# Moving the attention output step behind the gate arithmetic in a fused attention and SwiGLU kernel

## The chip, the cores and the metric

The kernel runs on one core of a Trainium2 chip. The core has five engines that work at the same time, each with its own instruction queue that it goes through in order: TensorE (PE in the profile; its weight loads are the row PEld), VectorE (DVE), ScalarE (ACT), GpSimd (POOL) and SyncE (SP, which here only issues transfers). They wait for each other through semaphores. Matmuls write to PSUM, a small memory of banks; DVE and ACT read the results from there.

The metric is the device time of one execution in microseconds (us). For the kernel before, three runs gave a median of 332.81 us, from 332.54 to 332.84.

## The reference

Two stages are computed one after the other. The first is attention with a hash mask, for 4 batches, 8 heads, 768 positions and 64 dimensions per head:

```
q_bits = (q @ proj > 0)                  # 6 bits per position; k_bits likewise
mask   = bucket(q_bits) == bucket(k_bits)
scores = where(mask, q @ k^T / 8, -1e9)
attn   = softmax(scores)                 # row sum + 1e-9 in the divisor
x      = attn @ v                        # heads side by side: 3072 tokens x 512
```

The second is a feed-forward block with RMS norm and a gate:

```
rms = sqrt(mean(x*x) + 1e-6)
xn  = x / rms * rms_g
out = (silu(xn @ w_gate) * (xn @ w_val)) @ w_out     # 512 -> 1536 -> 512
```

## The kernel before

The work is cut into 8 units of 384 query rows: batch u // 2, half u % 2. A unit has 8 heads, and a head takes 3 steps of scores. The program is written as a list of slots, NS = 24 for each unit and 8 * NS = 192 in all. A slot t issues `scores` (line 328) for step t + 1 on TensorE, `probs` (line 343, the exponential on ScalarE) for step t, and then every step that the list `plan[t]` holds, in the order in which the steps were put in with `at`. Each engine gets its instructions in this order, so the order of the list is the order of the queues. There is no other planner behind it.

These are the steps in the plan that matter here:

- `av` (line 352) multiplies the probabilities of a head with v into `o_ps`. A pair of heads shares one `o_ps` tile, and the pool that holds it has one buffer, so the next pair can start only when `o_ps` has been read. For head number n of the order, `av` runs in slots 3n + 4 and 3n + 5.
- `o_step` calls `attn_out` (line 368). Once a pair of heads is complete, in the slot of its last `av`, DVE reads `o_ps` into `otmp` (line 374), takes the reciprocal of the row sums, `rcp` (line 379), and POOL multiplies both to `x` (line 381). POOL then squares `x` into `sq` (line 387). In units 0 and 7 the last pair has all of this on DVE, with three instructions that square and sum at once (line 390).
- `s_step` calls `sumsq` (line 395), a DVE sum of `sq` into `ssp`. It comes five slots after `o_step`, and two slots after it for the last pair of a unit.
- `norm` (line 415) sums `ssp` on DVE (`ss`, line 408), lets POOL compute `rstd` (line 412), and scales `x` to `xn` on DVE (line 423). It stands in slot 4 of the next unit's 24 slots. `turn_x` (line 425) turns `xn` on TensorE (`x_ps`) and writes it back through DVE (`xnT`).
- `gate` and `value` (lines 449 and 458) are the first two matmuls of the feed-forward block, each in two parts of two matmuls. After the second part of `gate`, ScalarE takes a tanh of `g_ps` into `t` (line 455). After the second part of `value`, DVE forms `a` from `t` and `g_ps` (line 464) and `ht` from `a` and `v_ps` (line 465). Those two reads free the banks of `g_ps` and `v_ps`.
- `project` (line 471) is the last matmul, into `y_ps`; `store` copies it out and sends it off.
- `hash_one` (line 281) computes the mask bits of a head pair (matmuls into `d_ps`, DVE `bits`, eight transfers), and `turn_dve` (line 182) turns q and k on DVE. `v_mean` (line 313) makes `cvb`.

The tiles `g_ps`, `v_ps`, `y_ps`, `x_ps`, `d_ps` and `m_ps` all come from one pool of three PSUM banks (`bank`, line 83), used in turn. A `value` that follows a `gate` needs the bank that was used three tiles earlier.

The feed-forward work of unit u is spread over the 24 slots of unit u + 1 by `spread` (line 732): first the nine `project` pieces of unit u - 1 with the turns of `xn`, then the 48 pieces of `gate` and `value`. The plan is filled in this order: early steps, then `av`, `o_step` and `s_step` of all pairs in the loop from line 687 on, then `norm` and the pieces of `spread` with the inserted `hash_one` and `v_mean`, and last the turns, casts and loads (line 787 on). So within one slot DVE meets `otmp`, `rcp` and a row sum ahead of that slot's `a` and `ht`, and these ahead of `bits` and the turns.

A slot with number s has the place s % 24 in its unit. `o_step` of the pairs 0 to 3 stands at places 8, 14, 20 and, in the next unit's slots, 2. `s_step` stands at 13, 19, 1 and 4.

Of the kernel before, what the change touches and what calls it, by code (L numbers as in the profile page):

```python
# [8 lines left out]
FP32 = mybir.dt.float32  # L9
# [24 lines left out]
def kernel(  # L34
# [12 lines left out]
    nc = tc.nc  # L47
# [9 lines left out]
    spool = ctx.enter_context(tc.tile_pool(name="spool", bufs=2))  # L57
# [268 lines left out]
    x, xn, xnT = {}, {}, {}  # L326
# [41 lines left out]
    def attn_out(u, hp, eng=nc.gpsimd):  # L368
        b = u // 2
        if hp == 0:  # L370
            x[u] = xpool.tile([128, 3, DMODEL], FP32, name="x")
        o = ot.pop((u, hp))
        tmp = spool.tile([128, 3, 2, 66], FP32, name="otmp")
        nc.vector.tensor_add(  # L374
            tmp[:, :, :, 0:65], o[:, :, :, 0:65],
            cvb[b % 2][:, 2 * hp : 2 * hp + 2, 0:65].unsqueeze(1).to_broadcast([128, 3, 2, 65]),
        )
        r = spool.tile([128, 3, 2, 1], FP32, name="rcp")
        nc.vector.reciprocal(r, tmp[:, :, :, 64:65])  # L379
        xd = x[u][:, :, 128 * hp : 128 * hp + 128]  # L380
        eng.tensor_mul(  # L381
            xd.rearrange("p c (h d) -> p c h d", h=2), tmp[:, :, :, 0:64],
            r.to_broadcast([128, 3, 2, 64]),
        )
        sq = spool.tile([128, 3, 128], FP32, name="sq")
        if eng is nc.gpsimd:
            eng.tensor_mul(sq, xd, xd)  # L387
            return sq
        for c in range(3):
            nc.vector.tensor_tensor_reduce(  # L390
                out=sq[:, c], in0=xd[:, c], in1=xd[:, c], scale=1.0, scalar=0.0,
                op0=ALU.mult, op1=ALU.add, accum_out=ssp[u % 2][:, hp, c : c + 1],
            )

    def sumsq(u, hp, sq):
        nc.vector.tensor_reduce(  # L396
            out=ssp[u % 2][:, hp, :], in_=sq, op=ALU.add, axis=AX.X
        )
# [156 lines left out]
    NS = 24  # L555
# [5 lines left out]
    def at(w, s, f, *a):  # L561
        plan[NS * w + s].append(lambda: f(*a))
# [116 lines left out]
    sqs = {}  # L679

    def o_step(u, hp, *eng):
        sqs[u, hp] = attn_out(u, hp, *eng)

    def s_step(u, hp):
        sumsq(u, hp, sqs.pop((u, hp)))

    for n, (u, h) in enumerate(order):
        t = 3 * n + 4 - ((u, h) == (0, H - 1))
        for part in range(2):
            at(0, t + part, av, u, h, part)  # L690
        if h % 2:
            if (u, h) == (0, H - 1):

                at(0, t + 1, o_step, u, h // 2, nc.vector)
                at(0, t + 1, norm_scale, u)
                at(0, t + 1, nc.vector.tensor_scalar_mul, gcol, gcol, float(DMODEL) ** 0.5)
                at(0, t + 2, hash_only, 1, 1)
                at(0, t + 2, hash_signs, 1, 1)
                at(0, t + 2, norm, u)
                at(0, TX-1, norm_third, u, 2, nc.scalar.mul)  # L700
                at(0, TX + 1, send_pair, 1, 1)
                for c in range(3):
                    at(0, TX, turn_x, u, c, c == 2)
                continue
            if (u, h) == order[-1]:
                at(0, t + 1, o_step, u, h // 2, nc.vector)
                continue
            at(0, t + 1, o_step, u, h // 2)
            at(0, t + (6 if h < 7 else 3), s_step, u, h // 2)

    hole = []

# [19 lines left out]
    def spread(t0, n, pieces):  # L732
        fixed = [SCORES + (AV if (t - 1) % 3 < 2 else 0) for t in range(t0, t0 + n)]
        extra = [(t, *inserts.pop(t)) for t in range(t0, t0 + n) if t in inserts]
        total = sum(fixed) + sum(p[0] for p in pieces) + sum(e[1] for e in extra)
        i, done = 0, 0
        for s in range(n):
            done += fixed[s]
            while i < len(pieces):
                weight, whole, steps = pieces[i]  # L740
                full = done + weight // 2 > total * (s + 1) // n
                if extra and whole and t0 + s >= extra[0][0] and (full or extra[0][1] > MEAN):
                    _, weight, *step = extra.pop(0)
                    at(0, t0 + s, *step)
                    done += weight
                    continue
                if full:
                    break
                done += weight
                for delay, *step in steps:  # L750
                    at(0, t0 + s + delay, *step)
                i += 1
        for _, _, *step in extra:
            at(0, t0 + n - 1, *step)
        assert i == len(pieces)

    for u in range(7):
# [11 lines left out]
        for i in range(9):  # L769
            c, n = divmod(i, 3)  # L770
            steps = [(0, project, u - 1, c, 4 * n, 4 * n + 4)]
# [6 lines left out]
                ]  # L778
        spread(t0, NS, pieces + gates)
    for t, (_, *step) in inserts.items():  # L780
        at(0, t, *step)

    def behind_norm(t):

        return t - t % NS + 7 if 1 <= t % NS < 7 else t

    for (b, hp), (load, kturns, qturns, _) in spots.items():
# [3 lines left out]
        for w, turns in (("k", kturns), ("q", qturns)):  # L791
            for i, t in enumerate(turns):
                at(0, t, turn_dve, b, hp, w, i, len(turns))
            t = turns[-1] + 1
            at(0, t if (b, hp) == (1, 2) else behind_norm(t), cast_pool, b, hp, w)
        t = 54 if (b, hp) == (1, 2) else behind_norm(qturns[-1] + 2)
# [66 lines left out]
```

## Time and profile before

| what | value |
|---|---|
| median of the runs | 332.81 us |
| the profiled execution's own time | 333.62 us |
| its span, first to last instruction | 331.8 us |
| TensorE busy | 325.6 us |
| VectorE busy | 238.5 us |
| ScalarE busy | 227.1 us |
| GpSimd busy | 163.4 us |
| `otmp`, 32 instructions of 559 ns | 17.9 us |
| `sq` on POOL, 30 of 826 ns | 24.8 us |
| row sums `ssp`, 30 of 529 ns | 15.9 us |

The profile is of one execution, and its span leaves out 1.8 us of that execution's time. Busy time of TensorE is a sum over pipelined instructions whose ends are modelled, so it is the starts of matmuls that tell how fast TensorE goes: two matmuls in a row that start one matmul's time apart leave no gap. Times in the views of the trace count from the start of the span.

### The profile page before, as it was taken

The page shows a single profiled execution, that of the slowest core. Times are in us where ns is not written, and L with a number is a line of the kernel's source. Part 1 is how long each engine was busy: PE and PEld are TensorE (multiplying, and loading weights), DVE is VectorE, ACT ScalarE, POOL GpSimd, SP SyncE. Part 2 cuts the span into 40 slices and gives each one's busy share as a digit, 9 for nine tenths or more (in the row PEclk, how much of TensorE's full clock was granted, in tenths as well). Part 3 has the DMA queues.
Part 4 walks back from the last instruction along what each step waited for, and adds up shares of the span by engine and source line. Part 5 has one row for each costly group of instructions (what it writes and reads, how often), then busy time and mean ns, then how long its engine had stood idle before and what let it go on. Part 6 is the DMA issues. An engine that isn't in the chain of part 4 may idle for free.

```text
span 331.8 us, 7843 instructions
## 1 busy us (share of the span) xinstructions
PE 325.6 (98%) x2998; PEld 196.8 (59%) x2999; DVE 238.5 (72%) x496; ACT 227.1 (68%) x331; POOL 163.4 (49%) x210
## 2 busy tenths in 40 slices
PE   9999999999999999999999999999999999999995
PEld 3576666656565565656566565655656566665553
DVE  5887876859887668867888478886767356675860
ACT  6899887666777667775778667776767767744331
POOL 3999759965974734625574523556461111111000
PEclk9999999999999999999999999999999999999999
DMA  7942999987139554332816036001000010002002
GB/s 212 355 154 68 231 214 197 184 164 141 68 55 162 110 118 94 62 87 76 168 18 134 36 89 120 6 3 68 34 4 2 28 63 9 0 2 95 3 0 96
DMA packets 79613, 30.93 MB, mean 93 GB/s; under 512 B 64908, under 2 KB 76632, under 8 KB 79576
## 3 DMA queue, kind: packets, MB, share of 16 engines
q1 hardware_dynamic: 75672, 25.65, 32.8%
q0 software_dynamic: 3680, 4.72, 8.4%
q8 instruction: 23, 0.38, 0.5%
q14 instruction: 14, 0.11, 0.1%
q10 hardware_dynamic: 224, 0.07, 0.1%
HBM read 28.32 MB, written 6.29 MB: 104 GB/s over the span
## 4 chain that ended last, share of the span: by engine, by line
PE 93%; DVE 2%; ACT 1%; POOL 1%; DMA 1%; issue 0%; SPq 0%; POOLq 0%
PE s_ps L335 19%; PE v_ps L447 18%; PE g_ps L447 18%; PE y_ps L476 17%; PE o_ps L360 10%; PE t_ps L155 2%; PE d_ps L215 2%; PE d_ps L235 2%; PE x_ps L430 2%; PE z_ps L543 1%; DVE xn L423 1%; ACT psb L347 1%; PE y_ps L495 1%; DMA qL<-in_q_dram 1%; PE m_ps L319 0%
## 5 line engine op out<-in xcount | busy, mean ns | idle before, releaser
L347 ACT ACTIVATE psb<-s_ps,ebias 128x768 f16<-128x768 f32 x192 | 167.7, 899 | 21.1 <-PE s_ps L335 20.0
L335 PE MATMUL s_ps<-QK 128*128 128x384 f16 (+1 forms) x384 | 93.6, 326 | 1.2 <-ACT psb L347 1.1
L455 ACT ACTIVATE t<-g_ps 128x384 f32<-128x384 f32 x96 | 47.1, 491 | 54.5 <-PE g_ps L447 53.8
L447 PE MATMUL g_ps<-xnT,wg 128*128 128x384 f16 x384 | 82.7, 326 | 0.0
L447 PE MATMUL v_ps<-xnT,wv 128*128 128x384 f16 x384 | 81.8, 326 | 0.4 <-DVE a L464 0.2
L464 DVE SCALAR_TENSOR_TENSOR a<-t,g_ps 128x384 f32<-128x384 f32 x96 | 52.8, 550 | 26.3 <-ACT t L455 24.9
L476 PE MATMUL y_ps<-wo,ht 128*128 128x512 f16 x276 | 68.1, 379 | 0.0
L381 POOL TENSOR_TENSOR x<-otmp,rcp 128x384 f32<-128x384 f32 x30 | 25.1, 836 | 86.4 <-DVE rcp L379 86.0
L465 DVE SCALAR_TENSOR_TENSOR ht<-a,v_ps 128x384 f16<-128x384 f32 x96 | 53.2, 554 | 11.6 <-PE v_ps L447 3.1
L360 PEld LDWEIGHTS <-psb 128*128 128x128 f16 x1152 | 51.9, 97 | 15.7 <-issue 1.3
L360 PE MATMUL o_ps<-vl,psb 128*128 128x65 f16 x1152 | 55.8, 193 | 0.0
L335 PEld LDWEIGHTS <-QK 128*128 128x128 f16 (+1 forms) x384 | 34.5, 98 | 34.6 <-issue 9.2
L447 PEld LDWEIGHTS <-wv 128*128 128x128 f16 x384 | 35.3, 97 | 22.7 <-issue 2.0
L447 PEld LDWEIGHTS <-wg 128*128 128x128 f16 x384 | 34.7, 97 | 20.9 <-DVE xnT L436 0.4
L476 PEld LDWEIGHTS <-ht 128*128 128x128 f16 x276 | 24.8, 98 | 22.4
L488 ACT COPY ysb<-y_ps 128x512 f32<-128x512 f32 x23 | 13.5, 585 | 19.7 <-PE y_ps L476 19.7
L387 POOL TENSOR_TENSOR sq<-x 128x384 f32<-128x384 f32 x30 | 24.8, 826 | 2.4
L207 POOL CAST QK<-qT 64x768 f16<-64x768 f32 x20 | 16.4, 821 | 17.7 <-DVE qT L194 17.1
L374 DVE TENSOR_TENSOR otmp<-o_ps,cvb 128x390 f32<-128x390 f32 x32 | 17.9, 559 | 10.0 <-PE o_ps L360 9.8
L396 DVE TENSOR_REDUCE ssp<-sq 128x3 f32<-128x384 f32 x30 | 15.9, 529 | 7.9 <-POOL sq L387 7.8
L207 POOL CAST QK<-kT 64x768 f16<-64x768 f32 x20 | 16.4, 820 | 9.0 <-DVE kT L194 7.1
L423 DVE TENSOR_SCALAR xn<-x,rstd 128x512 f16<-128x512 f32 x23 | 15.8, 739 | 6.8 <-POOL rstd L412 6.8
(83 smaller groups left out, 283.1 us busy)
## 6 DMA issues: line engine op xcount, KB each, us to landing
vn<-in_v_dram SPq DMA_DIRECT2D x16, 384.0 KB
out_dram<-ysb SPq DMA_DIRECT2D x23, 256.0 KB
qL<-in_q_dram SPq DMA_DIRECT2D x40, 96.0 KB
kL<-in_k_dram SPq DMA_DIRECT2D x40, 96.0 KB
kn<-in_k_dram SPq DMA_DIRECT2D x5, 384.0 KB
qn<-in_q_dram SPq DMA_DIRECT2D x5, 384.0 KB
wg<-in_moe_w_gate_dram POOLq DMA_DIRECT2D x2, 768.0 KB, 9.5
wv<-in_moe_w_val_dram POOLq DMA_DIRECT2D x2, 768.0 KB, 11.8
```

What stands on the lines that cost most here:

```text
L207: nc.gpsimd.tensor_copy(QK[b, 2 * hp + hh, "h"][0:64, o : o + S], src[64 * hh : 64 * hh + 64, :])
L335: nc.tensor.matmul(ps[:, j, 0:HALF], QK[b, h, "h"][rows, S + jt * 128 : S + (jt + 1) * 128], QK[b, h, "h"][rows, half * HALF : (half + 1) ...
L347: nc.scalar.activation(psb[u, h][:, 2 * ch : 2 * ch + 2, :], sps.pop((u, i))[:, :, 0:HALF], AF.Exp, bias=ebias, scale=ESCALE,)
L360: nc.tensor.matmul(o[:, c, hh, 0:65], psb[u, h][:, jt, c * 128 : (c + 1) * 128], vls[b % 2][:, h, 2 * (jt % 3) + jt // 3 if b in PARITY el ...
L381: eng.tensor_mul(xd.rearrange("p c (h d) -> p c h d", h=2), tmp[:, :, :, 0:64], r.to_broadcast([128, 3, 2, 64]),)
L387: eng.tensor_mul(sq, xd, xd)
L423: mul(xn[u][:, c, :], x[u][:, c, :], rstds[u][:, c : c + 1])
L447: nc.tensor.matmul(ps, w[:, kt, fs], xnT[u][:, kt, :], start=(kt == 0), stop=(kt == 3))
L455: nc.scalar.activation(t, fbank[u, ft, "g_ps"], AF.Tanh, scale=0.5)
L464: nc.vector.scalar_tensor_tensor(out=a, in0=t, scalar=1.0, in1=g, op0=ALU.add, op1=ALU.mult)
L465: nc.vector.scalar_tensor_tensor(out=ht[u][:, ft, :], in0=a, scalar=0.5, in1=vv, op0=ALU.mult, op1=ALU.mult)
L476: nc.tensor.matmul(y, ht[u][:, ft, c * 128 : (c + 1) * 128], wo[:, ft, :], start=(ft == 0), stop=(ft == NF - 1),)
```

## The change

In the loop that plans `av`, `o_step` and `s_step`, steps in slots below 48, and those at places 2 and 4 of a unit, are put into the plan as before. All others are kept in a list and put in after the pieces of `spread` and the inserted steps, but still ahead of the turns, casts and loads. So in these slots `otmp`, `rcp`, `x`, `sq` and the row sums come behind that slot's `a`, `ht`, `bits` and `cvb` in the queues. TensorE's own order stays as it was.

The last pair of units 1 to 6 no longer squares on POOL. Its `s_step` instead issues the three DVE instructions that square and sum in one, reading `x`.

```
-        sq = spool.tile([128, 3, 128], FP32, name="sq")
-        if eng is nc.gpsimd:
+        if eng is nc.gpsimd and hp < 3:
+            sq = spool.tile([128, 3, 128], FP32, name="sq")
             eng.tensor_mul(sq, xd, xd)
             return sq
+        if eng is nc.vector:
+            sumsq_dve(u, hp)
+
+    def sumsq_dve(u, hp):
+
+        sq = spool.tile([128, 3, 128], FP32, name="sq")
+        xd = x[u][:, :, 128 * hp : 128 * hp + 128]
         for c in range(3):
             nc.vector.tensor_tensor_reduce(
...
     def s_step(u, hp):
-        sumsq(u, hp, sqs.pop((u, hp)))
-
+        sq = sqs.pop((u, hp))
+        if sq is None:
+            sumsq_dve(u, hp)
+        else:
+            sumsq(u, hp, sq)
+
+    late = []
...
-            at(0, t + 1, o_step, u, h // 2)
-            at(0, t + (6 if h < 7 else 3), s_step, u, h // 2)
+
+            steps = [(t + 1, o_step), (t + (6 if h < 7 else 3), s_step)]
+            for s, step in steps:
+                if s < 2 * NS or s % NS in (2, 4):
+                    at(0, s, step, u, h // 2)
+                else:
+                    late.append((s, step, u, h // 2))
...
     for t, (_, *step) in inserts.items():
         at(0, t, *step)
+
+    for t, *step in late:
+        at(0, t, *step)
```

## The prediction

> **What bounds the kernel now.** I read the page's busy times and clock first, then the chain of work that ended last, then the costliest groups.
>
> ```profile
> PE 325.6 (98%) x2998; PEld 196.8 (59%) x2999; DVE 238.5 (72%) x496; ACT 227.1 (68%) x331; POOL 163.4 (49%) x210
> PEclk9999999999999999999999999999999999999999
> PE 93%; DVE 2%; ACT 1%; POOL 1%; DMA 1%; issue 0%; SPq 0%; POOLq 0%
> L447 PE MATMUL v_ps<-xnT,wv 128*128 128x384 f16 x384 | 81.8, 326 | 0.4 <-DVE a L464 0.2
> ```
>
> TensorE carries 93% of the chain at full clock. The change gives it no work and takes none away, so it can only move the gaps between matmuls. The group row shows almost none (0.4 us), yet that idle time is counted against modelled, overlapping ends. I therefore measure gaps from start to start. The chain in order of time gives the price of a group without a gap:
>
> ```profile
> 79.30 0.86 PE y_ps L476 x4
> 81.14 0.65 PE v_ps L447 x4
> ```
>
> A 384-column matmul costs 0.1625 us (0.65 / 4), a 512-column one 0.216 us. The timeline from slot 48 on (span 67 us) was then searched for starts that lie further apart. Here are slots 163 to 165, with some lines left out:
>
> ```profile
> 252.30 0.49 PE L447 MATMUL v_ps<-xnT,wv 128*128 128x384 f16 x2
> ...
> 252.50 0.49 ACT L455 ACTIVATE t<-g_ps 128x384 f32<-128x384 f32 x1 [0.73 <-PE g_ps L447]
> ...
> 253.22 0.49 PE L447 MATMUL v_ps<-xnT,wv 128*128 128x384 f16 x2
> 253.42 0.56 DVE L374 TENSOR_TENSOR otmp<-o_ps,cvb 128x390 f32<-128x390 f32 x1 [0.40 <-PE o_ps L360]
> 253.55 0.81 PE L447 MATMUL g_ps<-xnT,wg 128*128 128x384 f16 x4
> 254.02 0.19 DVE L379 RECIPROCAL rcp<-otmp 128x6 f32<-128x6 f32 x1
> 254.13 0.52 DVE L464 SCALAR_TENSOR_TENSOR a<-t,g_ps 128x384 f32<-128x384 f32 x1
> 254.20 0.49 PE L335 MATMUL s_ps<-QK 128*128 128x384 f16 x2
> ...
> 254.70 0.81 PE L447 MATMUL v_ps<-xnT,wv 128*128 128x384 f16 x4
> 254.75 0.56 DVE L465 SCALAR_TENSOR_TENSOR ht<-a,v_ps 128x384 f16<-128x384 f32 x1
> ```
>
> The last `v_ps` should start 2 x 0.1625 after `s_ps`, at 254.52. It starts at 254.70, 0.05 us after `a` ends (254.13 + 0.52): it needs the bank of the `g_ps` that `a` reads. That `a` had its `t` at 252.99, but stood in the queue behind `otmp`, for which DVE even sat idle 0.40 us. This is what the change reorders.
>
> **Moving the output step.** Of the 18 moved `o_step`s, eight move past nothing on DVE: their slots (place 8 of every unit, 62, 188) issue no second `value` part and no `bits`. The other ten (68, 86, 92, 110, 116, 134, 140, 158, 164, 182) put `a` and `ht` first, and in 86 and 134 `bits` too. Five of the ten are followed by the gap above, `s_ps` to `v_ps` in the timeline: slot 69, 99.56 to 100.25, 0.365 us beyond the two matmuls; slot 93, 137.93 to 138.43, 0.175; slot 141, 215.18 to 215.69, 0.185; slot 159, 244.24 to 244.75, 0.185; slot 165, 0.175. The sum is 1.085 us. In each, `a` now starts 0.5 to 1.1 us sooner, so I take all of it.
>
> What is late next: `a` and `ht` of the following tile come behind `otmp` and `rcp`. In slot 69: qT's turn ends 99.15, `a` to 99.7, `ht` to 100.3, `otmp` to 100.9, `rcp` to 101.1, next `a` to 101.55. TensorE, free of its gap, asks for that bank at 101.78 at the earliest (after `v_ps`, `g_ps`, `s_ps` and nine `av`, which take 0.27 from 252.95 on: 99.88 + 0.65 + 0.65 + 0.33 + 0.27). The cover is 0.2 us; without it the part missing becomes a gap.
>
> Slot 135 has the sixth gap: four `g_ps` start at 206.32, the next `v_ps` at 207.27, so 0.30 us beyond 0.65. It waits for `ht`, which itself stood 0.46 us for a TensorE signal although its `v_ps` was done. Bounds are 0 and 0.30 gained; neither row is nearer, so I take 0.15.
>
> In slots 86, 110, 116 and 182 nothing is gained; there `otmp` is only later. Its reader is the next `av`, since `o_ps` has one buffer. Slot 110: `a` (167.81) cannot go sooner, its `t` ends 167.77; `ht` ends 169.02, `otmp` 169.5, `av` of slot 112 starts 169.68. Slot 182: `ht` ends 283.22, `otmp` 283.7, `av` 283.88. Slots 86 and 134, with `bits`: about 0.2 left likewise. The others leave 0.6 us or more. Nothing is charged while 0.2 holds (a DVE result reached TensorE in 0.05 above); at most I allow 0.1 at each of the four, 0.4.
>
> `x` and `sq` start 0.5 to 1.9 us later at the ten places. Behind them in POOL's queue stand casts and `vl` copies of later slots; POOL is 49% busy, and the row sum that needs `sq` is five slots away (8 us at some 1.6 per slot). Zero. SP's queue keeps its order; `bits` comes no later, so its eight transfers don't either. Zero.
>
> **Moving the row sums.** They take the same 0.53 us behind `a` and `ht`; nobody waits before `norm`. One exception: in slots 73, 97 and 145 (place 1, with `hash_one`) DVE idles before `bits` (0.39 us in slot 73), and the sum that filled that time now runs after it. It pushes `otmp` of slots 74, 98, 146, and the norm behind it, back by 0.5 us.
>
> **Squares on DVE.** Slots 123 to 125:
>
> ```profile
> 187.58 0.83 POOL L381 TENSOR_TENSOR x<-otmp,rcp 128x384 f32<-128x384 f32 x1 [2.25 <-DVE rcp L379]
> 188.49 0.83 POOL L387 TENSOR_TENSOR sq<-x 128x384 f32<-128x384 f32 x1
> ...
> 189.35 0.55 DVE L396 TENSOR_REDUCE ssp<-sq 128x3 f32<-128x384 f32 x1 [1.44 <-POOL sq L387]
> 189.94 0.17 DVE L408 TENSOR_REDUCE ss<-ssp 128x3 f32<-128x15 f32 x1
> ...
> 190.62 1.02 PE L476 MATMUL y_ps<-wo,ht 128*128 128x512 f16 x4
> 191.63 0.40 PE L430 MATMUL x_ps<-ident,xn 128*128 128x128 f16 x4
> ```
>
> From the end of `x` (188.41) to `ss` is 1.53 us. The new form is in the trace, in unit 0:
>
> ```profile
> 40.64 0.29 DVE L390 CUSTOM_DVE_ANT_0 sq<-x 128x128 f32<-128x128 f32 x1
> ...
> 41.40 0.17 DVE L408 TENSOR_REDUCE ss<-ssp 128x3 f32<-128x15 f32 x1
> ```
>
> That is 0.76 us for three squares and their reads, plus 0.05 to hear from POOL: 0.81, so the norm comes 0.72 sooner. In the units whose sum was pushed back 0.2 is left. In unit 1 DVE is held by `bits` until 72.67 in any case, and 72.67 + 0.76 is the 73.40 of before: nothing. TensorE waits for this chain in three places: slot 125 (191.63 instead of 190.62 + 4 x 0.216, 0.15 us), slot 103 (eight `x_ps` from 154.99 to `y_ps` at 155.55, where four take 0.23 from 191.63 on: 0.10) and slot 55 (77.89 to 78.54, 0.19, unit 1). I take 0.15, 0 and 0; bounds are 0.25 gained (all but unit 1's) and, for unit 1, 0.05 lost to rounding of the two forms. DVE's extra 0.2 us per unit falls in its 1.44 us wait.
>
> **Sum.** 1.085 + 0.15 + 0.15 = 1.38 us. Against the profiled execution (331.8 span, 333.62 with what lies around it) that is 332.24. The median of the runs lies 0.81 lower, so I predict 332.81 - 1.38 = **331.4 us**. Bounds of this case: 1.085 + 0.30 + 0.25 = 1.64 gained (331.2), or 1.085 - 0.4 - 0.05 = 0.63 (332.2). The tail after slot 192 is TensorE at its rate, so a gap removed is time removed.
>
> **Rivals.**
>
> *The banks stay short.* Only three PSUM banks serve these tiles, and `v_ps` follows `g_ps` at once. If the next `a` is late by what this one gains, each gap reappears one tile on. For it: the cover above is 0.2 us, smaller than slot 69's gap. Against it: the gaps follow the `otmp` slots alone; between them the same ring runs gapless. If four fifths of the gain return, 0.28 is left: 332.5. The Trainium skill, "Perfetto Trace Analysis" (Identifying Performance Opportunities, Optimization Strategy), reads one gap that repeats on the saturated engine as a possible lack of PSUM for the next tile, which speaks for this rival. The trace agrees that four gaps of some 0.18 us repeat; that `a` could have started 1.1 us before it did says the order, not the count of banks.
>
> *The accumulator becomes the wait* (slower). `otmp` now waits for whatever `ht` waits for, and the next `av` waits for `otmp`. At the four thin places 0.15 us is free after the signal. A delay of 0.46, the row of slot 134, costs 4 x 0.31 = 1.24 and eats the gain. From 0.67 on the kernel is slower by over 0.2%; at 0.92, twice that row, it costs 3.1, net 1.7: 334.5. For it: that unexplained 0.46. Against it: it occurs once, and in before these places had over 2 us to spare.
>
> *The squares get in each other's way.* If each DVE square sequence sits behind a POOL operation of 0.83 us, the norm is 0.1 later instead of 0.72 sooner, and 0.8 in unit 1: 0.8 + 5 x 0.1 lost, no 0.15 gained, so 332.81 - 1.23 + 1.3 = 332.9. For it: three `xn` took 2.77 us beside POOL's casts (74.56) but 1.28 without (191.09). Against it: POOL has nothing between `x` and `rstd` there. The Trainium skill, "SBUF — State Buffer" (two separate sides), says a DVE operation with two SBUF inputs and a GpSimd operation exclude each other for a whole instruction; that would be the cause here.
>
> **How the numbers follow.** Forecast 0.70 (331.2 to 332.2), banks 0.15, accumulator 0.11, squares 0.04. Changes under 0.2% (0.67 us) can't be told from none here. So faster 0.70, same 0.15 + 0.04 = 0.19, slower 0.11. The range leaves out the accumulator and 0.05 below: 330.9 to 332.9.
>
> **What would show it.** Slots 69, 93, 141, 159, 165: `v_ps` 0.33 after `s_ps`, `a` ahead of `otmp`. Slot 125: `x_ps` 0.86 after `y_ps`. Wrong if starts of `o_ps` in slots 88, 112, 136, 184 come after a gap and behind `otmp`, if `v_ps` gaps appear a tile later, or if `ss` comes more than 0.9 after `x`.

## The result and the profile after

The changed kernel takes 331.09 us, the median of six runs (330.52 to 331.68), against 332.82 us before (six runs, 332.54 to 333.57). The ratio is 0.9944, with a 95% interval of 0.9928 to 0.9960: faster by 0.4 to 0.7%. The forecast was 331.4. The profiled execution took 330.52 us and has a span of 328.7 us.

From the page of the changed kernel, its busy times, the clock, the shares of the chain, and the group of `v_ps` (busy time, mean ns | idle time before):

```profile
PE 323.0 (98%) x2999; PEld 196.6 (60%) x2999; DVE 239.5 (73%) x526; ACT 227.2 (69%) x331; POOL 158.4 (48%) x204
PEclk9999999999999999999999999999999999999999
PE 97%; ACT 1%; issue 0%; DVE 0%
L454 PE MATMUL v_ps<-xnT,wv 128*128 128x384 f16 x384 | 81.8, 326 | 0.0
```

TensorE still does the same work at full clock. Its share of the chain rose from 93 to 97%, and the idle time ahead of `v_ps`, 0.4 us before, is gone. Lines from 390 on are numbered seven higher than before. Slots 163 to 165 in the timeline, some lines left out:

```profile
249.78 0.49 ACT L462 ACTIVATE t<-g_ps 128x384 f32<-128x384 f32 x1 [0.73 <-PE g_ps L454]
...
250.30 0.55 DVE L471 SCALAR_TENSOR_TENSOR a<-t,g_ps 128x384 f32<-128x384 f32 x1
...
251.03 0.56 DVE L472 SCALAR_TENSOR_TENSOR ht<-a,v_ps 128x384 f16<-128x384 f32 x1 [0.17 <-PE v_ps L454]
...
251.48 0.49 PE L335 MATMUL s_ps<-QK 128*128 128x384 f16 x2
251.50 0.56 DVE L374 TENSOR_TENSOR otmp<-o_ps,cvb 128x390 f32<-128x390 f32 x1
...
251.81 0.81 PE L454 MATMUL v_ps<-xnT,wv 128*128 128x384 f16 x4
```

`a` starts 0.03 us after its `t` ends (250.27), where it stood 1.14 us before; `otmp` comes behind `ht`; and the last `v_ps` starts 0.33 us after `s_ps` (251.81 - 251.48), which is two matmuls of 0.1625. The gap of 0.175 us is closed. The norm of slots 123 to 125:

```profile
185.71 0.83 POOL L381 TENSOR_TENSOR x<-otmp,rcp 128x384 f32<-128x384 f32 x1 [2.25 <-DVE rcp L379]
...
186.58 0.29 DVE L397 CUSTOM_DVE_ANT_0 sq<-x 128x128 f32<-128x128 f32 x1 [0.53 <-POOL x L381]
...
187.34 0.18 DVE L415 TENSOR_REDUCE ss<-ssp 128x3 f32<-128x15 f32 x1
...
188.76 1.02 PE L483 MATMUL y_ps<-wo,ht 128*128 128x512 f16 x4
...
189.62 0.39 PE L437 MATMUL x_ps<-ident,xn 128*128 128x128 f16 x4
```

From the end of `x` (186.54) to `ss` it is 0.80 us instead of 1.53, and `x_ps` follows `y_ps` after 0.86 us, four matmuls of 0.216, without a gap.

To see all gaps at once I compared the start of the first `scores` matmul of each slot in both traces, from slot 47 on. Where this difference steps down, a gap was closed. The steps of 0.05 us and more, for this kernel and for the first four experiments, in us against the kernel before:

| slot of the gap | predicted | changed kernel | order only | squares only | six moved | all but six moved |
|---|---|---|---|---|---|---|
| 55 | 0 | -0.07 | | -0.07 | | |
| 59 | | | +0.53 | | | |
| 69 | -0.365 | -0.38 | -0.38 | | -0.38 | |
| 93 | -0.175 | -0.18 | -0.18 | | -0.18 | |
| 102 and 103 | 0 | -0.11 | +0.47 | -0.12 | | +0.47 |
| 125 | -0.15 | -0.15 | | -0.15 | | |
| 135 | -0.15 | -0.30 | -0.30 | -0.30 | -0.30 | |
| 141 | -0.185 | -0.19 | -0.19 | | -0.19 | |
| 159 | -0.185 | -0.18 | -0.19 | | -0.18 | |
| 163 | | | | +0.33 | | |
| 165 | -0.175 | -0.18 | -0.18 | | -0.18 | |
| slot 47 to the last matmul | -1.38 | -1.77 | -0.43 | -0.35 | -1.42 | +0.48 |

The spans differ by 3.1 us (331.8 to 328.7), more than these 1.77. Some 0.1 lies in slots before 48 and 0.2 behind the last matmul; the other 1.0 is the start: the first `scores` matmul began 8.00 us into the span in the profiled execution before, 6.99 in the one after. In two later traces of the changed order that first `scores` began at 7.72 and 7.62 us, so this 1.0 is scatter of the start and not the change.

### The profile page after: what moved, and what is told of

It is laid out like the page before. It is cut to its first block, busy times and chain, and to the rows that moved or that the text cites. A ratio compares the mean times of both kernels' runs of the same rounds, so it can differ in the third digit from the quotient of the medians.

```text
span 328.7 us, 7869 instructions
## 1 busy us (share of the span) xinstructions
PE 323.0 (98%) x2999; PEld 196.6 (60%) x2999; DVE 239.5 (73%) x526; ACT 227.2 (69%) x331; POOL 158.4 (48%) x204
## 4 chain that ended last, share of the span: by engine, by line
PE 97%; ACT 1%; issue 0%; DVE 0%
PE s_ps L335 20%; PE g_ps L454 19%; PE v_ps L454 19%; PE y_ps L483 18%; PE o_ps L360 11%; PE d_ps L215 2%; PE t_ps L155 2%; PE d_ps L235 2%; PE x_ps L437 2%; PE z_ps L550 1%; ACT psb L347 1%; PE y_ps L502 1%; PE m_ps L319 1%; DVE kT L157 0%; PE s_ps L155 0%
## 5 line engine op out<-in xcount | busy, mean ns | idle before, releaser
L387 POOL TENSOR_TENSOR sq<-x 128x384 f32<-128x384 f32 x24 | 19.8, 826 | 1.9
L443 DVE TENSOR_TENSOR xnT<-x_ps,gcol 128x512 f16<-128x512 f16 x22 | 14.5, 686 | 8.0 <-PE x_ps L437 7.9
```

## The experiments

**The two parts alone.** The first pair separates the reordering from the squares.

```
 e1_order_only, from the changed kernel:
-        if eng is nc.gpsimd and hp < 3:
+        if eng is nc.gpsimd:
 e2_squares_only, from the changed kernel:
-                if s < 2 * NS or s % NS in (2, 4):
+                if True:
```

> The reordering alone; all pairs but the last of units 0 and 7 square on POOL as before. Order theory (a gate's `a` stood behind `otmp` and kept its bank): the six gaps ahead of `v_ps` in slots 69, 93, 135, 141, 159 and 165 close, 1.4 us from start to start. The row sums of slots 73, 97 and 145 still run after `bits` and push the norm 0.5 us back, with no faster squares to make up for it, so slot 103 loses 0.3 to 0.5 and slots 55 and 125 keep their gaps: net 1.0 us, about 331.8. Bank theory (three banks too few): the gaps reappear one tile on, and the kernel is at 332.5 or more.

> The squares on DVE alone; every step stays in its old place in the queue. Order theory: the six `v_ps` gaps stay at 1.4 us in sum. The norm of units 2 to 6 comes 0.72 us sooner and closes slots 103 and 125 (0.10 to 0.12 and 0.15 us), slot 55 at most by 0.07: 0.3 us gained, 332.5, hardly to be told from no change by the clock, but to be seen in the starts. If the six gaps closed here, the squares and not the order would be their cause.

Measured: the order alone 331.68 us (331.35 to 332.22), ratio 0.9963 [0.9952, 0.9975]; the squares alone 332.41 us (332.17 to 333.40), ratio 0.9990 [0.9981, 0.9999]. The order carries most of the gain, the squares a little, and the two support one another. With the order alone the norm of unit 3 comes late and costs 0.47 us in slots 102 and 103. With the squares as well the same place gains 0.11. The squares alone close the gaps 55, 103 and 125, as in the changed kernel, and two entries in their column were expected by nobody: slot 135 closes although `otmp` was not moved, and slot 163 opens. They are taken up below.

The trace of the order alone also has a wait that neither kernel shows, in slot 59:

```profile
80.30 5.71 SPq L294 DMA_DIRECT2D QK<-bits  x7
...
83.42 0.48 PE L335 MATMUL s_ps<-QK 128*128 128x384 f16 x2 [0.36 <-DMA QK<-bits]
```

The mask bits of pair (1,2) stand on SP's queue behind nine loads of slot 50. Here their transfers are issued from 80.30 us on. The wait shows in two later traces as well, where they were issued from 79.95 (the wider order: 0.10 us) and from 80.60 (POOL squares too: 0.99 us). It shows in no trace in which they were issued by 79.49, nor in the one with sixteen writes at the head of DVE's queue, where slot 59 itself came later (issued from 80.37).

**Which of the moved steps matter.** Next only the six `o_step`s at the predicted gaps were moved, or all but these six. POOL squares in both of these.

```
 e3_six_only (beside the edit of e1):
-                if s < 2 * NS or s % NS in (2, 4):
+                if step is s_step or s not in (68, 92, 134, 140, 158, 164):
 e4_all_but_six (beside the edit of e1):
-                if s < 2 * NS or s % NS in (2, 4):
+                if s < 2 * NS or s % NS in (2, 4) or (step is o_step and s in (68, 92, 134, 140, 158, 164)):
```

> Only the six output steps of slots 68, 92, 134, 140, 158 and 164 are moved; squares and row sums as before. Order theory: 1.4 us gained in six steps of 0.37, 0.18, 0.30, 0.18, 0.18 and 0.18, and nothing elsewhere: 331.4. A theory by which the gain comes from a general relief of DVE or POOL over all 18 moved steps expects a third of it, 332.3.

> The complement: all steps moved but the six output steps of slots 68, 92, 134, 140, 158 and 164; squares as before. Order theory: the six gaps stay, nothing is gained; the row sums of slots 73, 97 and 145 behind `bits` push the norm back 0.5 us and cost 0.3 to 0.5 at slot 103: 333.1 to 333.3. General relief: two thirds of the gain, 331.9. Accumulator theory: starts of `av` behind `otmp` in slots 88, 112 and 184, 0.3 us each.

Measured: the six alone 331.19 us (331.14 to 331.47), ratio 0.9948 [0.9937, 0.9960]; all but six 333.43 us (332.97 to 334.21), ratio 1.0015 [1.0006, 1.0024]. Six moved steps give the whole gain of the order, and by the clock they can't be told from the whole change (331.09 and, in a later run, 331.36). The other twelve `o_step`s and all the row sums give nothing and cost 0.48 us where POOL squares. In the trace of all but six, DVE and TensorE around slots 99 to 103:

```profile
149.76 0.55 DVE L403 TENSOR_REDUCE ssp<-sq 128x3 f32<-128x384 f32 x1 [1.51 <-POOL sq L387]
...
151.50 2.76 DVE L430 TENSOR_SCALAR xn<-x,rstd 128x512 f16<-128x512 f32 x3 [0.98 <-POOL rstd L419]
```
```profile
154.28 0.39 PE L437 MATMUL x_ps<-ident,xn 128*128 128x128 f16 x4
154.91 0.38 PE L437 MATMUL x_ps<-ident,xn 128*128 128x128 f16 x4 [0.24 <-DVE xnT L443]
```

The late row sum pushes the norm, and TensorE waits for its result. The squares on DVE make up for it: in the changed kernel nothing of this remains. The sum is right too: the six moved steps (-1.42) and the norm's three places (-0.07 - 0.11 - 0.15 = -0.33) are the -1.77 of the changed kernel, to 0.02.

**The accumulator as the wait.** `otmp` frees `o_ps`, the one buffer into which the next `av` writes. The distance from the end of `otmp` to that `av` fell from 2.07 to 0.15 us in slot 86, from 2.04 to 0.19 in slot 110 and from 2.16 to 0.19 in slot 182. Slot 110 of the changed kernel:

```profile
167.07 0.56 DVE L374 TENSOR_TENSOR otmp<-o_ps,cvb 128x390 f32<-128x390 f32 x1
...
167.81 0.35 PE L360 MATMUL o_ps<-vl,psb 128*128 128x65 f16 x6
```

`otmp` ends at 167.63, `av` starts at 167.81. To see what lies behind this edge, the moved `o_step`s were put one slot later:

```
 e5_one_slot_later, from the changed kernel:
-                    late.append((s, step, u, h // 2))
+                    late.append((s + (step is o_step), step, u, h // 2))
```

> The changed kernel with every moved output step one slot later still, behind the gate arithmetic of slots 9, 15 and 21. Accumulator theory: `otmp` now ends after the next `av` wants its only buffer. In slot 69 `ht` ends 1.4 us behind the `otmp` of the changed kernel, in slots 111 and 159 likewise 1 to 1.5, against 0.15 to 1.4 us to spare, so most of the 18 places open a gap of 0.3 to 1.3 us ahead of `av`: 8 to 18 us slower than the changed kernel, 340 to 349. If `o_ps` did not decide, it would stay within 1 us of 331.1.

Measured: 344.06 us (two runs, 343.61 and 344.52), ratio 1.0334 [1.0316, 1.0352]. Its list of TensorE's waits (total, times, longest) begins:

```profile
PE o_ps L360 <- DVE otmp L374: 10.3, 15, 1.4
```

Fifteen waits of up to 1.4 us, and none in the changed kernel. The rival is real, and one slot away.

**Earlier and wider.** If moving pays from slot 48 on, it might from slot 36 on; and the row sums at place 1 might better stay ahead of `bits`.

```
 e6_wider, from the changed kernel:
-                if s < 2 * NS or s % NS in (2, 4):
+                if s < 36 or s % NS in (1, 2, 4):
```

> The changed kernel with the reordering begun at slot 36 instead of 48 (it takes in the output steps of slots 38 and 44), and with the row sums at place 1 left in front of `bits` as before. Order theory: the gap of 0.16 us in slots 44 and 45 (`g_ps` to `v_ps`) closes, the norm of units 2, 3 and 5 comes 0.5 us sooner without a use for it, the rest stays: 330.9, not to be told from the changed kernel by the clock, but to be seen in the starts. Nothing can become slower by it unless an `av` starts behind `otmp` in slots 40 or 46.

Measured: 331.86 us (331.29 to 332.79), ratio 0.9968 [0.9955, 0.9982]. The expectation was missed. Slots 55, 103 and 125 gain what they gain in the changed kernel, so the place of those row sums has no effect with the squares on DVE. Moving the `o_step`s between slots 36 and 47 closed no gap there and opened a new one, in slot 45:

```profile
58.89 0.55 DVE L472 SCALAR_TENSOR_TENSOR ht<-a,v_ps 128x384 f16<-128x384 f32 x1
...
59.36 0.56 DVE L374 TENSOR_TENSOR otmp<-o_ps,cvb 128x390 f32<-128x390 f32 x1
59.79 0.81 PE L454 MATMUL g_ps<-xnT,wg 128*128 128x384 f16 x4
...
60.06 0.52 DVE L471 SCALAR_TENSOR_TENSOR a<-t,g_ps 128x384 f32<-128x384 f32 x1
60.63 0.48 PE L454 MATMUL v_ps<-xnT,wv 128*128 128x384 f16 x2
```

Four `g_ps` from 59.79 end their turn at 60.44, but `v_ps` starts at 60.63, 0.05 after `a` ends (60.58): `otmp` now sits in front of the next tile's `a`. That is the rival of the short banks, with 0.19 us, at a place that the change leaves alone. The trace also has 0.32 us in slot 49, a wait of `y_ps` for the transfer of `wo`, and 0.10 us in slot 59.

**Squares against POOL.** The shared access that the third rival needs does not occur in the changed kernel, since POOL has nothing between `x` and `rstd`. Here POOL is given the old square again, into a tile that nobody reads, beside DVE's.

```
 e7_pool_squares_too, from the changed kernel:
+        if eng is nc.gpsimd:
+            eng.tensor_mul(spare, xd, xd)
```

> The changed kernel, in which POOL squares `x` of the last pair too, into a tile that nobody reads, at the same time as DVE does. If a POOL operation that reads SBUF keeps DVE from two SBUF inputs for a whole instruction, one of the two waits: the three squares take 0.76 + 0.83 us or POOL's starts only behind a square, and `ss` comes up to 1.6 us after the end of `x` instead of 0.79. If not, `ss` stays at 0.8 us and POOL's 0.83 us run beside it. In the time: 0 to 0.5 us slower, for the norm would come as late as before.

Measured: 331.74 us (331.50 to 332.74), ratio 0.9970 [0.9960, 0.9980]. The squares of unit 3's norm, in its timeline:

```profile
149.39 0.29 DVE L399 CUSTOM_DVE_ANT_0 sq<-x 128x128 f32<-128x128 f32 x1 [0.60 <-POOL x L381]
149.43 0.93 POOL L390 TENSOR_TENSOR spare<-x 128x384 f32<-128x384 f32 x1
...
149.61 0.91 DVE L399 CUSTOM_DVE_ANT_0 sq<-x 128x128 f32<-128x128 f32 x1
```

The second square takes 0.91 us instead of 0.28: it ends 0.16 us behind POOL's multiplication (150.52 against 150.36), and `ss` comes 1.41 us after `x` instead of 0.80. Slots 102 and 103 lose 0.35 us instead of gaining 0.11. (This trace also holds the 0.99 us of slot 59, which belong to the transfers and not to the squares.) The mechanism of the rival is as the Trainium skill has it ("SBUF — State Buffer", two separate sides: a DVE operation with two SBUF inputs and a GpSimd operation that reads SBUF exclude each other for a whole instruction); with these rows, 0.63 us is what it takes. Its condition was missing from the change.

**The gap of slot 135.** In the kernel before, `ht` of slot 134 stood 0.46 us. The trace names a `s_ps` matmul, which `ht` does not read, and the `v_ps` that it does read had ended at 205.27:

```profile
206.32 0.81 PE L447 MATMUL g_ps<-xnT,wg 128*128 128x384 f16 x4
206.66 0.56 DVE L465 SCALAR_TENSOR_TENSOR ht<-a,v_ps 128x384 f16<-128x384 f32 x1 [0.46 <-PE s_ps L335]
...
207.27 0.49 PE L447 MATMUL v_ps<-xnT,wv 128*128 128x384 f16 x2
```

With the squares alone nothing there is moved, and the gap is gone; but an `ht` in slot 163 has the same 0.46 us now, and it is TensorE's new wait:

```profile
250.43 0.55 DVE L472 SCALAR_TENSOR_TENSOR ht<-a,v_ps 128x384 f16<-128x384 f32 x1 [0.46 <-DVE a L471]
...
251.03 0.48 PE L454 MATMUL v_ps<-xnT,wv 128*128 128x384 f16 x2 [0.17 <-DVE ht L472]
```

If DVE's records are numbered from 0 in order of start, its waits for semaphores included, the late `ht` of before is number 447, and that of the squares alone is number 575, 128 further on. In the order alone and in the six moved, number 447 is a wait that belongs to `bits`, and it too starts 0.40 us after the record ahead of it. So the pause belongs to the place in DVE's queue, not to the instruction. Two experiments add sixteen instructions on DVE to the kernel before and move nothing. Each writes a 128 x 3 tile sixteen times more, the first at the head of the queue, the second at the end of slot 121, where DVE has 2.42 us to spare.

```
 e8_sixteen_more, from the kernel before:
-    nc.vector.memset(mhalf, -0.5)
+    for _ in range(17):
+        nc.vector.memset(mhalf, -0.5)
 e12_sixteen_in_a_wait, from the kernel before:
+    def extra():
+        for _ in range(16):
+            nc.vector.memset(fill3, 0.0)
+
+    at(0, 121, extra)
```

> The kernel before with 16 memsets of 60 ns more at the head of DVE's queue, and nothing moved. In before and in the run with all steps moved but six, `ht` of slot 134 stands 0.46 us for no producer, and it is the 447th instruction of DVE (counted from 0, with its event waits); in the two runs that moved slot 134, the 447th is an event wait of `bits`, and that stands 0.4 us. Position theory: the pause belongs to the place in the queue, so with 16 more instructions it falls on what was the 431st, where DVE waits anyway, and the 0.30 us gap in slot 135 closes though `otmp` is still ahead of `a`: 332.6 to 332.8 (0.2 for the memsets at most). Order theory for this slot: the gap stays.

> The kernel before, with sixteen writes of a small unused tile (128x3, some 0.06 us each) on DVE at the end of slot 121, where DVE then idles 2.42 us ahead of the next `otmp`; nothing is moved. Theory (the 0.30 us gap of slot 135 comes from a pause of DVE at a fixed number of instructions, so any sixteen more ahead of it put the pause on another instruction, one with slack): the gap of slot 135 closes (0.30 us), everything up to slot 121 stays as before, and the start is not touched: 332.5 to 332.7 us, a ratio of 0.9985 to 0.9995. Rival (the 0.30 us of slot 135 belong to `ht`'s own operands): the gap stays and the time is that of before, 332.8 to 333.0 us. As the sixteen are the same number as in the run that had them at the head of the queue and took 334.45 us, a time near 332.6 us also says that its loss lay in the start and not in the shift.

In both traces slot 135 closes by 0.298 us, the only step between slot 47 and the last matmul (-0.335 us in all, both times). In the second, with the line numbers one higher:

```profile
205.74 0.81 PE L448 MATMUL g_ps<-xnT,wg 128*128 128x384 f16 x4
...
206.39 0.49 PE L448 MATMUL v_ps<-xnT,wv 128*128 128x384 f16 x2
```

`v_ps` starts 0.65 after `g_ps`, where it took 0.95. In the first, number 447 is again a semaphore wait, with 0.42 us before it, and number 319 is an `ht` with 0.40. In the second, number 447 is a transpose that starts 0.41 us after the wait ahead of it, just as the `ht` that ran beside that wait ends. That part of the theory is shown. The times, though, were missed in both: 334.45 us (333.78 to 335.12), ratio 1.0052 [1.0036, 1.0068], and 333.01 us (332.55 to 333.55), ratio 1.0008 [0.9999, 1.0017]. The profiled executions tell where the 0.33 us went: what lies around the span is 2.13 us in the first (333.78 less 331.65) and 2.14 in the second (332.99 less 330.85), and 1.77 to 1.81 in the traces of all other kernels here; the other runs of the two kernels agree (2.08 to 2.18). What lengthens it is open; it isn't DVE's number of instructions, since the changed kernel has more records on DVE (708 against 696 and 695) and 1.78. The first kernel's further loss, 1.44 us from median to median, lies in the start, as far as one trace can tell. Each write lasts 0.06 us, but they start 0.128 us apart, so sixteen hold DVE for 2 us and not for 1. DVE copies `kT` only at 5.65 us, where it did so at 4.11 in the second kernel, and TensorE waits for that copy:

```profile
6.36 0.51 PE L235 MATMUL d_ps<-kT,pj 64*32 64x384 f32 x2 [1.46 <-DVE kT L157]
```

The first `scores` came at 8.34 us, the latest of all traces.

**The loads ahead of `bits`.** Since some traces show the wait in slot 59, the loads of the projection step (2,0) were put three slots later, behind the transfers, in both kernels; the changed kernel ran beside them once more.

```
 e9_loads_later (changed kernel) and e10_before_loads_later (kernel before):
-        (2, 0): (50, (63, 64, 65, 66), (67, 69, 70, 71), 73),
+        (2, 0): (53, (63, 64, 65, 66), (67, 69, 70, 71), 73),
 e11_changed_again: no edit
```

> The changed kernel, with the loads of the projection step (2,0) issued at slot 53 and not at slot 50, so that they stand behind the eight `bits` transfers of pair (1,2) on SP's queue and no longer ahead of them. Theory (the transfers of slot 51 land late in some executions because nine loads stand ahead of them on the queue): no wait for `QK<-bits` in slot 59, 330.6 to 331.0 us, and times nearer to one another than those of the changed kernel. Rival (the scatter of the times comes from the start-up and not from this queue): 331.1 us, no narrower. A second rival: the loads now come late for the steps of unit 2, which begin at slot 63; then a new wait for kL or qL stands there, and the time is 331.5 us or more.

> The kernel before, with the loads of (2,0) issued at slot 53 and not at slot 50, nothing else. The kernel before reaches slot 51 at the same distance from its loads as the changed kernel. Theory: it gains no more than the changed kernel does by the same edit, so 332.5 to 332.9 us; its trace showed no wait in slot 59. Rival (loads late for slot 63): 333.2 us or more.

> The changed kernel once more, unaltered, beside the other two on one chip: 331.1 us, a ratio of 0.993 to 0.996 to the kernel before. It is what e9 is held against.

Measured: 331.39 us (330.89 to 331.87), ratio 0.9961 [0.9947, 0.9975]; the kernel before with the edit 332.66 us (332.13 to 333.04), ratio 0.9991 [0.9981, 1.0001]; the changed kernel again 331.36 us (330.73 to 331.84), ratio 0.9956 [0.9939, 0.9972]. The edit moves the transfers from 79.38 to 72.32 us and no new wait appears, yet time and scatter stay: the theory fell, the rival (the scatter is in the start) stands. Three traces of the changed order (the result's, e9, e11) need 262.99 us from slot 47's `scores` to the end of the last matmul in each, while the first `scores` came at 6.99, 7.72 and 7.62 us and the times were 330.52, 331.41 and 331.35. The kernel before with the edit gained its 0.30 us of slot 135 as well, where its number 447 is now another record. No variant beats the changed kernel beyond its interval.

## Why the prediction was right

The forecast, 331.4, lies 0.3 us above the first median measured, 331.09, and beside that of the later run, 331.36; the mechanism that it named is the one that the runs show. Step by step:

- *The five gaps, 1.085 us.* They closed by 1.11 (0.38 + 0.18 + 0.19 + 0.18 + 0.18), and the six moved steps alone show that it is these. Taking the whole of each gap was right because `a` had been ready long before.
- *What is late next.* In slot 69 the cover was put at 0.2 us; it was 0.47 (`a` ended at 100.12, `v_ps` asked at 100.59). No gap came back a tile later. The rival of the banks failed for that reason, not because it can't happen: slot 45 shows it as soon as the `o_step`s ahead of slot 48 are moved. There the wait is one for a bank, which the Trainium skill's reading of repeated gaps ("Perfetto Trace Analysis", Optimization Strategy) names as a possible cause. Whether a fourth bank would close it was not run; the five gaps of the change were closed by the order alone, with the same three banks.
- *Slot 135, 0.15 of 0 to 0.30.* The term was mis-sized: it gave 0.30. The reason was not seen. The prediction called the 0.46 unexplained, and rightly priced both ends; it belongs to a place in DVE's queue, and edits that only shift the queue removed it. This part of the gain is luck of the numbering, and the squares alone lost it again in slot 163. What the order would give there with the pause still in place was not run.
- *The squares, 0.15.* Slot 125 gave 0.15 as predicted, and `x` to `ss` took 0.80 against 0.81. The two terms taken as zero were mis-sized: slot 103 gave 0.11 and slot 55 0.07. For slot 103 the text contradicted itself, leaving the norm 0.2 sooner and yet charging no gain; for slot 55 it let the squares wait for the end of `bits`, and in the trace the first starts 0.08 us before that end.
- *The row sums at place 1 push the norm by 0.5.* Right: with POOL's squares they cost 0.47 us. That the squares pay for it was right too.
- *The thin places.* 0.2 us was forecast at four; 0.15, 0.19 and 0.19 were measured at three, and slot 134 kept 0.47. Nothing was charged, and nothing was lost. One effect was not foreseen: `otmp` of slot 188 moves past nothing, as the text said, but the row sum of slot 187, now behind its slot's `a` and `ht`, has come to stand right ahead of it, and its distance fell from 1.44 to 0.98, at no cost.
- *POOL's and SP's queues, zero.* No wait for either appears in the changed kernel.
- *The sum.* 1.38 was predicted, 1.77 measured in the trace: 0.15 + 0.11 + 0.07 from the three mis-sized terms, and rounding. Setting the sum against the median instead of the profiled execution was right: that execution had begun its first `scores` at 8.00 us, later than in every other trace but the one with sixteen writes at its head.

## What to carry to other kernels

Where one engine is the bound, measure its gaps from start to start and ask of each what its releaser had been ready for; if the releaser stood in its own queue behind work that nobody waited for, the order is worth a try, and only the steps in front of those gaps matter. Before moving a step that frees a single buffer, compute the time left to its next writer: here it went from 2 us to 0.15, and one slot more cost 13 us. A gap without a producer may hang on the number of instructions ahead of it; don't credit an edit with closing it until an edit that only shifts the queue has been tried.

## What the hardware showed besides

- DVE pauses 0.40 to 0.42 us at certain numbers of its queue, 319, 447 and 575 where they were seen, 128 apart: number 447 in six of the kernels, on an `ht` in two and on a semaphore wait in four. Each time a short semaphore wait stood just ahead. Behind a long instruction the pause costs nothing: in the changed kernel none shows, and with the output steps one slot later number 447 starts 0.41 us after the `ht` ahead of it started, while that `ht` (0.55 us) still runs. The numbers are not exact: in the squares alone a semaphore wait at number 318 starts 0.43 us after such an `ht`. The Trainium skill ("Runtime: NRT & Kernel Launch", Instruction fetch mechanics) says that an engine's instructions are refilled in blocks of 256 and that a crossing is mostly hidden. Half such a block fits the spacing, and hidden behind a long instruction fits what is seen; that the refill is the cause was not tested.
- A square of 128 x 128 on DVE went from 0.28 to 0.91 us beside one POOL multiplication, which itself took 0.93 instead of 0.83.
- Sixteen tiny DVE writes made the time around the span some 0.33 us longer in both kernels that had them, by a cause that stays open. They last 0.06 us each and start 0.128 us apart.
